# Step 1 to step 2 of the first batch by copies within SBUF for four of sixteen groups, and a new order of the prologue and the first chunk

## The chip, the core and the metric

One core of a Trainium2 chip. It has a matrix engine (TensorE, here PE, whose weight loads are shown as PEld), three others that compute (VectorE, DVE; ScalarE, ACT; GpSimd, POOL), SyncE (SP), which here only issues DMAs, and DMA engines that all queues share. SBUF is the memory on the chip, PSUM the one that PE writes to. The metric is the time of one execution on the device, in microseconds (us).

## The reference

```python
def reference(x, g_ln, w1, w2):                 # x: 8 x 3136 x 256
    x = np.fft.fft(np.fft.fft(x, axis=1), axis=2).real.astype(np.float32)
    mu = np.mean(x, axis=-1, keepdims=True)
    var = np.mean((x - mu) ** 2, axis=-1, keepdims=True)
    xn = (x - mu) / np.sqrt(var + 1e-06) * g_ln
    return x + np.maximum(xn @ w1, 0.0) @ w2    # w1: 256 x 1024, w2: 1024 x 256
```

The weights arrive as 64-bit floats, and the kernel reads them as pairs of 32-bit words.

## The kernel before

The Fourier transform over the 3136 positions of a batch is done in two steps, as 3136 = 64 x 49. Step 1 transforms over 64; the input is folded by symmetry, so that 25 of the 49 residues are left, which stand in 14 slots in two halves. Seven pieces i of two slots each pass through it: `load_x(b, i)`, `fold_zw` (DVE in the first batch), `step1` (PE, lines 247 and 249), a copy from PSUM to the tile `s1` (ACT, line 257). `s1` has the 64 results of both halves on its 128 partitions and slot, half and column in the free dimension. Step 2 contracts over the slots and eight of the partitions; so the data has to change its layout: `store1` (line 261) writes a piece to the tensor `scratch` in HBM, 256 KB each, and `relayout` (line 268) reads it back to the tile `s2` with slot and r on the partitions (8 x 14 = 112), and the 16 groups g (partition p = 16 r + g of `s1`) in the free dimension. In the trace `s1` and `s2` are both called s. `step2(m, ...)` (line 301) takes two groups of `s2` and the table `tab_s`, part "m" on PE; "h" and "f" are ACT's copies to the chunk's tiles (lines 321 and 323), "l" is DVE's low part (line 325).

What follows is done in 49 chunks c of 256 columns, each with 8 steps f of the hidden dimension, s = 8 c + f. `moe1_a(s)` multiplies with `w1` (six matmuls, line 345, three passes of high and low parts), which then already has the transform over the 256 columns in it; ACT copies one half (line 350), DVE makes both halves of h (lines 351 and 352). `moe1_b(s)` rounds h to its high part (ACT, line 359) and takes the rest as low part (DVE, line 360). `moe2(s)` multiplies with `w2` (twelve matmuls, line 395). `residual` (line 419) and its followers add x and the normalisation; `finish` (lines 468 and 470) and `store_out` write the result.

In the main loop, from s = 6 on, PE does `moe1_a(s)`, then `moe2(s - 3)`; `late` and `after` hold what else is due at a step, among it the folds, step 1 and the relayout of the next batch (in batch 1 the relayout is due after s = 34, its first step 2 after s = 45).

Before the loop stands a prologue whose order is written out by hand for PE, ACT, DVE, POOL and SP (lines 661 to 794). Beside step 1 of the first batch it makes the weights ready, in four quarters of each. For a quarter of w1: `convert_m` (DVE, lines 509 and 511), `convert_z` (ACT, line 517), `convert_b` (DVE, lines 522 and 524), `finish_w1` (DVE, line 552); then, for each half, `transform_w1` (PE, line 562, four matmuls to the profile for a call), `round_w1` (ACT, line 570), `rest_w1` (PE, line 575) and `rest_w1_copy` (ACT, line 580). For a quarter of w2, which is loaded to the place of the same quarter of w1 (`load_w2`): the same three conversions, `finish_w2` (DVE, line 584), and `split_w2`: the high part on ACT (line 528), the low part on POOL (line 529). `warm_up` runs matmuls on zeros.

Each engine does its instructions in order, and a wait of one holds all that stand behind it on that engine, DMA issues on its queue among them.

## Time and profile before

| | us |
|---|---|
| three timed runs | 1022.9, 1023.34, 1023.9 |
| their median | 1023.34 |
| profiled execution, its time | 1021.02 |
| profiled execution, its span | 1019.2 |

| engine | busy us in the span | share |
|---|---|---|
| PE | 1005.3 | 99% |
| DVE | 813.2 | 80% |
| ACT | 540.4 | 53% |
| POOL | 244.4 | 24% |

The span is from the first to the last instruction of the program; the time of that execution is 1.8 us longer. A row of the profile names the line of the kernel, the engine, the operation, the tiles (output <- inputs), the shapes, and in brackets the idle time of the engine before it and what ended that. A DMA row is the issue; its landing is told separately. PE's matmuls are pipelined, so the distance of two starts says what one costs.

### The profile page before, as it was taken

What the parts mean: (1) busy time and instruction counts of PE and PEld (TensorE: products, weight loads), DVE (VectorE), ACT (ScalarE), POOL (GpSimd) and SP (SyncE); (2) the same over time, 40 slices, a digit from 0 to 9 for tenths busy, and PEclk for the clock granted to TensorE, in tenths of its full rate; (3) what the DMA queues carried; (4) which work ended last, traced back from release to release, by engine and by line L of the source; (5) the groups of instructions that cost most, each with busy time, mean ns of one, the idle gap of its engine ahead of it and who ended that gap; (6) DMA issues with size and microseconds to landing.
All of it is one profiled execution on the core that took longest, in us unless ns stands there. A gap on an engine that the chain in (4) does not pass through costs nothing.

```text
span 1019.2 us, 21749 instructions
## 1 busy us (share of the span) xinstructions
PE 1005.3 (99%) x8279; PEld 984.7 (97%) x8280; DVE 813.2 (80%) x2190; ACT 540.4 (53%) x1416; POOL 244.4 (24%) x278
## 2 busy tenths in 40 slices
PE   9889999999999999999999999999999999999998
PEld 6779999999999999999999999999999999999998
DVE  7687887778787877878887887878788778878887
ACT  3545545655555455555456545555555554455453
POOL 2136504430154203341043401442024300000000
PEclk9999999999999999999999999999999999999999
DMA  9933343323222411243123132223101230100101
GB/s 348 265 129 105 105 125 104 103 74 104 74 83 94 146 52 53 85 135 104 43 89 119 66 105 81 83 94 122 56 30 46 73 104 23 42 22 22 43 22 42
DMA packets 41528, 92.10 MB, mean 90 GB/s; under 512 B 4176, under 2 KB 18704, under 8 KB 40528
## 3 DMA queue, kind: packets, MB, share of 16 engines
q1 hardware_dynamic: 40016, 88.87, 26.4%
q8 instruction: 66, 1.08, 0.4%
q0 software_dynamic: 320, 1.05, 0.3%
q10 hardware_dynamic: 1088, 0.79, 0.2%
q14 instruction: 38, 0.31, 0.1%
HBM read 50.32 MB, written 40.37 MB: 89 GB/s over the span
## 4 chain that ended last, share of the span: by engine, by line
PE 93%; DVE 4%; DMA 1%; ACT 1%; issue 0%; POOL 0%; SPq 0%; ACTq 0%; DVEq 0%
PE acc L395 52%; PE ab L345 26%; PE ps L301 5%; PE psy L419 4%; PE ps L254 3%; DVE h_lo L360 1%; PE ps L247 1%; PE ps L249 1%; DMA scratch<-s 1%; PE pw L659 1%; DVE h L351 1%; DVE h L352 1%; DMA s<-scratch 0%; ACT h_hi L359 0%; PE bb L345 0%
## 5 line engine op out<-in xcount | busy, mean ns | idle before, releaser
L395 PE MATMUL acc<-w_lo,h_hi 128*128 128x256 f32 x1568 | 438.5, 280 | 1.0 <-POOL w_lo L529 1.0
L395 PE MATMUL acc<-w_hi,h_lo 128*128 128x256 f32 x1568 | 438.5, 280 | 0.3 <-ACT w_hi L528 0.2
L395 PE MATMUL acc<-w_hi,h_hi 128*128 128x256 f32 x1568 | 438.6, 280 | 0.0
L360 DVE SCALAR_TENSOR_TENSOR h_lo<-h,h_hi 128x512 fp32r<-128x512 f32 x392 | 287.6, 734 | 173.3 <-ACT h_hi L359 171.4
L359 ACT ACTIVATE h_hi<-h 128x512 fp32r<-128x512 f32 x392 | 249.8, 637 | 259.6 <-DVE h L352 259.3
L395 PEld LDWEIGHTS acc<-w_lo,h_hi 128*128 128x128 f32 x1568 | 295.0, 188 | 1.2 <-POOL w_lo L529 1.2
L395 PEld LDWEIGHTS acc<-w_hi,h_lo 128*128 128x128 f32 x1568 | 295.3, 188 | 0.9 <-ACT w_hi L528 0.4
L395 PEld LDWEIGHTS acc<-w_hi,h_hi 128*128 128x128 f32 x1568 | 295.0, 188 | 0.0
L345 PE MATMUL ab<-ckl,w_hi 128*128 128x256 f32 x768 | 221.3, 288 | 2.3 <-DVE h L352 2.3
L345 PE MATMUL ab<-ckh,w_lo 128*128 128x256 f32 x768 | 216.7, 282 | 0.7 <-ACT w_lo L580 0.4
L345 PE MATMUL ab<-ckh,w_hi 128*128 128x256 f32 x768 | 215.5, 281 | 0.0
L217 POOL TENSOR_TENSOR fl<-f,fh 128x512 fp32r<-128x512 f32 x49 | 64.0, 1305 | 506.8 <-ACT fh L211 506.8
L351 DVE TENSOR_TENSOR h<-asb,ab 128x256 f32<-128x256 f32 x384 | 158.7, 413 | 1.9 <-ACT asb L350 1.9
L352 DVE TENSOR_TENSOR h<-asb,ab 128x256 f32<-128x256 f32 x384 | 158.7, 413 | 0.0
L345 PEld LDWEIGHTS ab<-ckl,w_hi 128*128 128x128 f32 x768 | 145.2, 189 | 6.2 <-issue 2.6
L350 ACT COPY asb<-ab 128x256 f32<-128x256 f32 x384 | 139.1, 362 | 19.8 <-PE ab L345 13.9
L345 PEld LDWEIGHTS ab<-ckh,w_lo 128*128 128x128 f32 x768 | 145.5, 189 | 3.3 <-ACT w_lo L580 0.6
L345 PEld LDWEIGHTS ab<-ckh,w_hi 128*128 128x128 f32 x768 | 145.7, 190 | 0.0
L321 ACT CAST ckh<-ps 128x392 fp32r<-128x392 f32 (+49 forms) x112 | 39.7, 356 | 66.6 <-PE ps L301 66.3
L257 ACT COPY s<-ps 128x508 f32<-128x508 f32 x56 | 32.7, 584 | 75.5 <-PE ps L254 62.5
L301 PE MATMUL ps<-tab_s,s 112*128 112x98 f32 (+1 forms) x512 | 65.6, 273 | 2.4 <-DMA s<-scratch 2.4
L301 PEld LDWEIGHTS ps<-tab_s,s 112*128 112x128 f32 x512 | 62.1, 192 | 2.9 <-issue 2.9
(108 smaller groups left out, 961.2 us busy)
## 6 DMA issues: line engine op xcount, KB each, us to landing
xs<-x SPq DMA_DIRECT2D x56, 512.0 KB, 4.3
out<-o SPq DMA_DIRECT2D x96, 256.0 KB, 2.4
scratch<-s SPq DMA_DIRECT2D x49, 256.0 KB, 2.1
s<-scratch SPq DMA_DIRECT2D x7, 1792.0 KB, 9.4
w1p_all<-w SPq DMA_DIRECT2D x8, 512.0 KB, 9.0
scratch<-s POOLq DMA_DIRECT2D x4, 256.0 KB, 6.4
s<-scratch SPq DMA_DIRECT2D x2, 448.0 KB, 5.4
s<-scratch SPq DMA_DIRECT2D x1, 896.0 KB, 12.1
```

The source lines that it names most:

```text
L217: nc.gpsimd.tensor_tensor(out=lo, in0=f, in1=hi.bitcast(F32), op=ALU.subtract)
L257: nc.scalar.copy(s[:, :, :, :127], ps[:, :, :, :127])
L301: nc.tensor.matmul(ps[:, h, k0 - base:k1 - base], s2[b][:KP, g, 128 * h:128 * h + 128], tab_s[:, h, k0:k1], start=(h == 0 and g == 2 * j), ...
L321: nc.scalar.copy(hi, src)
L345: nc.tensor.matmul(pt, wt[wi][:, j, fs], ch[xi][:, j, :w], start=(n == 0), stop=(n == 2))
L350: nc.scalar.copy(asb[:, :w], pa)
L351: nc.vector.tensor_tensor(out=h[:, :w], in0=asb[:, :w], in1=pb, op=ALU.add)
L352: nc.vector.tensor_tensor(out=h[:, w:], in0=asb[:, :m], in1=pb[:, :m], op=ALU.subtract)
L359: nc.scalar.activation(h_hi, h, AF.Relu)
L360: nc.vector.scalar_tensor_tensor(out=h_lo, in0=h, scalar=0.0, in1=h_hi.bitcast(F32), op0=ALU.max, op1=ALU.subtract)
L395: nc.tensor.matmul(acc[c, i][:, side], hs[xi][:, h0:h0 + 128], ws[wi][:, f], start=(f == 0 and side == 0 and n == 0), stop=(f == 7 and n = ...
L419: nc.tensor.matmul(ps[:, j, :129 + j], ck[:, j], ty_s[:, j, :129 + j], start=(j == 0), stop=True, skip_group_check=True)
```

## The change

Groups 0 to 3 of the first batch go from `s1` to `s2` by `direct`: for each group one DMA for the slots 0 to 9 (80 KB) and one for the slots 10 to 13 (32 KB), from eight partitions of `s1` to 80 or 32 of `s2`. For this the partitions of `s2` are ordered anew, in two parts with r outside and the slot inside, and the rows of the table `tab` with them; `relayout` becomes two DMAs, in all batches. The other twelve groups of the first batch and all later batches go by the scratch as before. The four copies of the first part are issued on POOL's queue after the last `ends`; the four of the second part in turn on ACT's and POOL's queue after the last `step1`. All stores of the first batch are issued by SP, after the loads of two quarters of w2. The relayout of the groups 0 to 3 and the warm-up ahead of step 2 are gone. `tw`, a part of `tab`, and `tz` are loaded earlier, w2 later. In the first chunk step 2 comes before the second half of w1 is transformed; the transform, its rounding and the conversions of w2 stand between the operations of the chunk, and `moe2` starts earlier in the order. The last quarter of w2 is converted in the steps 6 to 8 of the loop.

```diff
--- before.py
+++ after.py
@@ -39,6 +39,7 @@
 ROWS = NB * N
 NU = NS // 2
 KP = 8 * NS
+PARTS = (0, 10), (10, NS)
 
 
 def unit_k(unit):
@@ -94,7 +95,8 @@
                     else:
                         rows[:, 0, t:t + n], rows[:, 1, t:t + n] = ((c, s), (-s, c))[comp]
             t += n
-    tab = tab.transpose(3, 0, 1, 2, 4, 5).reshape(112, 2, HALF)
+    tab = tab.transpose(3, 0, 1, 2, 4, 5).reshape(NS, 8, 2, HALF)
+    tab = np.concatenate([tab[a:b].swapaxes(0, 1).reshape(-1, 2, HALF) for a, b in PARTS])
     tz = np.concatenate([tz.reshape(4 * NS, 50), np.zeros((KP - 4 * NS, 50))])
     d = np.arange(1, 129)[:, None]
     ang = 2 * np.pi * ((d * np.arange(129)) % D) / D
@@ -261,12 +263,21 @@
         in_order(eng.dma_start(scratch[b][2 * i:2 * i + 2].rearrange("s p d -> p s d"),
                                s.rearrange("p a h d -> p a (h d)")))
 
-    def relayout(b, g0=0, g1=16, eng=nc.sync):
+    def relayout(b, g0=0, g1=16):
         if b not in s2:
             s2[b] = work.tile([128, 16, D], F32, tag="s2", name=f"s2_{b}")
-        sv = scratch[b].rearrange("s (r g) d -> s r (g d)", g=16)
-        in_order(eng.dma_start(s2[b][:KP, g0:g1].rearrange("r g d -> r (g d)"),
-                               sv[:, :, g0 * D:g1 * D]))
+        sv = scratch[b].rearrange("s (r g) d -> r s (g d)", g=16)
+        for s0, e0 in PARTS:
+            in_order(nc.sync.dma_start(s2[b][8 * s0:8 * e0, g0:g1].rearrange("p g d -> p (g d)"),
+                                       sv[:, s0:e0, g0 * D:g1 * D]))
+
+    def direct(part, g0, g1, eng=nc.sync):
+
+        if 0 not in s2:
+            s2[0] = work.tile([128, 16, D], F32, tag="s2", name="s2_0")
+        s0, e0 = PARTS[part]
+        for g in range(g0, g1):
+            eng.dma_start(s2[0][8 * s0:8 * e0, g], s1[0][g:128:16, s0:e0])
 
     gb = group_bounds()
     chunk = {}
@@ -543,7 +554,7 @@
         nc.sync.dma_start(wp.rearrange("p (f d) -> p f d", f=2), w2v[:, 2 * n:2 * n + 2])
         w2p.append(wp)
 
-    gws = {}
+    gws, w2f = {}, []
 
     def finish_w1(n):
 
@@ -569,15 +580,13 @@
         for j in range(2):
             nc.scalar.copy(w1_cols(w1_hi, k, j), psw[k, j])
 
-    def rest_w1(k):
-
-        for j in range(2):
-            nc.tensor.matmul(psw[k, j], minus, w1_cols(w1_hi, k, j), start=False, stop=True,
-                             skip_group_check=True)
-
-    def rest_w1_copy(k):
-        for j in range(2):
-            nc.scalar.copy(w1_cols(w1_lo, k, j), psw.pop((k, j)))
+    def rest_w1(k, j):
+
+        nc.tensor.matmul(psw[k, j], minus, w1_cols(w1_hi, k, j), start=False, stop=True,
+                         skip_group_check=True)
+
+    def rest_w1_copy(k, j):
+        nc.scalar.copy(w1_cols(w1_lo, k, j), psw.pop((k, j)))
 
     def finish_w2(n):
         _, e, f = conv.pop(f"w2_{n}")
@@ -677,9 +686,11 @@
             load_w1(1)
             for i in (5, 6):
                 load_x(0, i)
+            nc.sync.dma_start(tw_all, tw)
             load_w1(2)
+            nc.sync.dma_start(tab_s[:, :, :gb[4]], tab[:, :, :gb[4]])
+            nc.sync.dma_start(tz_s, tz)
             load_w1(3)
-            nc.sync.dma_start(tw_all, tw)
             nc.gpsimd.memset(zmu, 0.0)
             nc.gpsimd.memset(masked, 0.0)
             ends(0, 0, 6)
@@ -693,12 +704,7 @@
             fold_zw(0, 2, nc.vector)
             step1(0, 2)
             convert_b("w1_0")
-            load_w2(0)
-            nc.sync.dma_start(tab_s[:, :, :gb[4]], tab[:, :, :gb[4]])
-            nc.sync.dma_start(tz_s, tz)
             step1_ends(0, 0, 6)
-            for i in range(3):
-                store1(0, i, nc.scalar if i % 2 else nc.gpsimd)
             ends(0, 6, 10)
             fold_zw(0, 3, nc.vector)
             step1(0, 3)
@@ -707,94 +713,105 @@
             step1(0, 4)
             finish_w1(0)
             step1_ends(0, 6, 10)
-            store1(0, 3, nc.scalar)
-            store1(0, 4, nc.gpsimd)
             ends(0, 10, NS)
+            direct(0, 0, 4, nc.gpsimd)
             convert_m("w1_1", w1p[1])
             fold_zw(0, 5, nc.vector)
             step1(0, 5)
             convert_z("w1_2", w1p[2])
             convert_b("w1_1")
+            load_w2(0)
             load_w2(1)
+            for i in range(5):
+                store1(0, i)
             fold_zw(0, 6, nc.vector)
             step1_ends(0, 10, NS)
-            store1(0, 5, nc.scalar)
+            store1(0, 5)
             step1(0, 6)
-            store1(0, 6, nc.gpsimd)
+            direct(1, 0, 1, nc.scalar)
+            direct(1, 1, 2, nc.gpsimd)
+            direct(1, 2, 3, nc.scalar)
+            direct(1, 3, 4, nc.gpsimd)
+            store1(0, 6)
             finish_w1(1)
+            nc.scalar.copy(minus, tw_all[:, 512:])
             convert_z("w1_3", w1p[3])
             convert_m("w1_2", w1p[2])
+            transform_w1(0, 0)
             convert_b("w1_2")
             finish_w1(2)
-            relayout(0, 0, 4)
-            relayout(0, 4, 8)
             load_w2(2)
             nc.sync.dma_start(tab_s[:, :, gb[4]:gb[8]], tab[:, :, gb[4]:gb[8]])
+            relayout(0, 4, 8)
             relayout(0, 8, 16)
-            nc.scalar.copy(minus, tw_all[:, 512:])
-            transform_w1(0, 0)
+            nc.sync.dma_start(ty_s, ty)
+            nc.sync.dma_start(tab_s[:, :, gb[8]:], tab[:, :, gb[8]:])
+            convert_m("w1_3", w1p[3])
+            convert_b("w1_3")
+            finish_w1(3)
+            load_w2(3)
+            for i in range(NU):
+                load_x(1, i)
             transform_w1(0, 1)
             round_w1(0)
-            convert_m("w1_3", w1p[3])
-            convert_b("w1_3")
-            load_w2(3)
-            nc.sync.dma_start(ty_s, ty)
-            nc.sync.dma_start(tab_s[:, :, gb[8]:], tab[:, :, gb[8]:])
-            for i in range(NU):
-                load_x(1, i)
-            finish_w1(3)
+            rest_w1(0, 0)
+            rest_w1_copy(0, 0)
+            convert_z("w2_0", w2p[0])
+            convert_m("w2_0", w2p[0])
+            convert_b("w2_0")
+            step2(0, "m")
+            rest_w1(0, 1)
+            step2(0, "h")
+            rest_w1_copy(0, 1)
+            step2(1, "m")
+            step2(0, "l")
+            f0 = finish_w2(0)
+            step2(1, "hl", 0)
+            convert_z("w2_1", w2p[1])
+            moe1_a(0, ((0, 0), (1, 0), (0, 1)))
+            moe1_a(1, ((0, 0), (1, 0), (0, 1)))
+            split_w2(0, f0)
             transform_w1(1, 0)
-            rest_w1(0)
-            convert_z("w2_0", w2p[0])
-            convert_z("w2_1", w2p[1])
-            rest_w1_copy(0)
+            convert_m("w2_1", w2p[1])
+            moe1_b(0)
+            step2(0, "f")
+            moe1_a(2)
+            moe1_b(1)
+            moe2(0)
             transform_w1(1, 1)
             round_w1(1)
-            convert_m("w2_0", w2p[0])
-            convert_b("w2_0")
-            f = finish_w2(0)
-            split_w2(0, f)
-            convert_m("w2_1", w2p[1])
             convert_b("w2_1")
-            warm_up(6, warm_h)
-            step2(0, "m")
-            step2(0, "hl")
-            step2(1, "m")
-            step2(1, "hl", 0)
-            f = finish_w2(1)
-            moe1_a(0, ((1, 0), (0, 0), (0, 1)))
-            split_w2(1, f)
-            step2(0, "f")
-            moe1_a(1, ((1, 0), (0, 0), (0, 1)))
-            rest_w1(1)
-            moe1_b(0)
-            moe1_a(2)
-            moe1_b(1)
+            moe1_a(3)
             moe1_b(2)
-            moe1_a(3)
-            rest_w1_copy(1)
+            f1 = finish_w2(1)
+            moe2(1)
+            rest_w1(1, 0)
+            rest_w1(1, 1)
+            split_w2(1, f1)
+            rest_w1_copy(1, 0)
+            rest_w1_copy(1, 1)
+            moe1_b(3)
+            step2(1, "hl", 1)
+            convert_a("w2_2", w2p[2])
+            moe1_a(4)
             step2(1, "f")
-            convert_a("w2_2", w2p[2])
-            step2(1, "hl", 1)
-            moe2(0)
-            moe1_b(3)
-            moe1_a(4)
+            moe2(2)
+            step2(2, "m")
+            moe1_b(4)
             convert_b("w2_2")
-            f = finish_w2(2)
-            split_w2(2, f)
+            f2 = finish_w2(2)
+            step2(2, "h")
+            moe1_a(5)
+            split_w2(2, f2)
+            step2(2, "l")
+            step2(2, "f")
             nc.gpsimd.tensor_scalar(out=neg, in0=ty_s[:, 1, 129:130], scalar1=2.0, scalar2=-1.0,
                                     op0=ALU.mult, op1=ALU.add)
-            moe2(1)
-            step2(2, "m")
-            moe1_b(4)
-            moe1_a(5)
-            step2(2, "hf")
-            step2(2, "l")
-            convert_a("w2_3", w2p[3])
-            moe2(2)
-            add_late(6, convert_b, "w2_3")
-            add_late(7, make_w2, 3)
-            add_late(8, split, t1_hi, t1_lo, tu_s[:, 0:128])
+            add_late(6, convert_a, "w2_3", w2p[3])
+            add_late(7, convert_b, "w2_3")
+            add_late(7, lambda: w2f.append(finish_w2(3)))
+            add_late(8, lambda: split_w2(3, w2f.pop()))
+            add_late(9, split, t1_hi, t1_lo, tu_s[:, 0:128])
 
         main.append(True)
         lag, last = 3, 8 * NCH
```

## Rows read from the trace of the kernel before

**Rows 1.** Windows: busy us (x instructions) by engine, granted clock, DMA share, GB/s.

```profile
28.90:33.20 4.30, 1.87 (x7) 0.59 (x6) 2.15 (x4) 3.14 (x6) 0.56 (x1) 1.00 0.88 228
33.20:39.40 6.20, 5.80 (x33) 5.52 (x34) 2.42 (x6) 2.65 (x8) 1.66 (x2) 0.72 1.07 265
...
48.20:60.00 11.80, 9.61 (x74) 8.71 (x73) 9.22 (x19) 7.12 (x20) 3.68 (x4) 1.00 0.61 241
...
100.00:1000.00 900.00, 899.12 (x7567) 892.08 (x7567) 722.45 (x1978) 485.79 (x1277) 209.23 (x231) 1.00 0.24 77
```

**Rows 2.** Timeline, 21 to 49 us: start, us, engine, line, names, idle before.

```profile
21.30 0.58 ACT L257 COPY s<-ps 128x508 f32<-128x508 f32 x1 [1.31 <-PE ps L249]
...
24.02 0.75 DVE L552 SCALAR_TENSOR_TENSOR gw<-fw,g_s,ew 128x512 f32<-128x512 f32 x1
...
28.31 0.80 SPq L268 DMA_DIRECT2D s<-scratch  x2
...
33.25 0.66 PE L301 MATMUL ps<-tab_s,s 112*128 112x99 f32 x4 [2.43 <-DMA s<-scratch]
...
35.82 0.57 PE L345 MATMUL ab<-ckh,w_lo 128*128 128x256 f32 x1 [0.35 <-ACT ckh L321]
...
48.20 0.29 PE L345 MATMUL ab<-ckl,w_hi 128*128 128x256 f32 x1
```

**Rows 3.** The chain of waits in order of time: start, us, what.

```profile
22.18 5.92 DMA scratch<-s
28.31 4.80 DMA s<-scratch
...
50.96 0.33 DVE h L351
```

**Rows 4.** Timeline of PE, 29 to 37 us: the warm-up, two matmuls of chunk 0.

```profile
29.58 1.24 PE L659 MATMUL pw<-warm_h 128*128 128x512 bf16 x5
...
36.40 0.41 PE L345 MATMUL ab<-ckl,w_hi 128*128 128x256 f32 x1
...
36.62 0.41 PE L345 MATMUL ab<-ckh,w_lo 128*128 128x256 f32 x1
```

**Rows 5.** DMA issues, whole run and (g_s) to 60 us: median to landing.

```profile
scratch<-s SPq DMA_DIRECT2D x49, 256.0 KB, 2.1
...
s<-scratch SPq DMA_DIRECT2D x7, 1792.0 KB, 9.4
...
g_s<-g_ln ACTq DMA_DIRECT2D x1, 1.0 KB, 3.6
```

**Rows 6.** Waits of SP's queue to 60 us: total, times, longest.

```profile
SPq L697 <- DMA scratch<-s: 5.9, 1, 5.9
```

**Rows 7.** Groups by line, 7 to 60 us: busy us, mean ns, idle before.

```profile
L562 PE MATMUL psw<-gw,tw_all 128*128 128x512 f32 x16 | 7.3, 599 | 0.7 <-DMA tw_all<-tw 0.7
...
L580 ACT CAST w_lo<-psw 128x512 fp32r<-128x512 f32 x4 | 2.1, 588 | 0.0
...
L350 ACT COPY asb<-ab 128x256 f32<-128x256 f32 x9 | 3.3, 367 | 2.4 <-PE ab L345 2.4
...
L524 DVE SCALAR_TENSOR_TENSOR ew<-w1p_all,ew 128x512 int32<-128x512 int32 x8 | 5.5, 692 | 0.3
...
L522 DVE TENSOR_SCALAR ew<-ew 128x512 int32<-128x512 int32 x8 | 3.4, 422 | 1.3 <-ACT ew L517 1.3
...
L529 POOL TENSOR_TENSOR w_lo<-fw,w_hi 128x512 fp32r<-128x512 f32 x4 | 5.1, 1286 | 30.8 <-ACT w_hi L528 30.8
```

**Rows 8.** Line 360 from 40 to 75 us: shortest, median, longest in ns.

```profile
L360 DVE SCALAR_TENSOR_TENSOR h_lo<-h,h_hi x13: 678/684/1367, 39.8 to 73.0; 128x512 fp32r<-128x512 f32 x13
```

**Rows 9.** Waits from 48.2 to 73.6 us: total, times, longest.

```profile
PE ab L345 <- DVE h L352: 1.4, 4, 0.6
...
PE psy L419 <- DVE o L470: 1.3, 1, 1.3
...
PE acc L395 <- POOL w_lo L529: 1.0, 1, 1.0
```

## The prediction

> **What bounds the kernel now.** I read the time by stretch first. From 100 to 1000 us TensorE (PE) is busy 899.12 of 900 us with 7567 matmuls at the full granted clock, 0.119 us each [rows 1]: nothing that this change touches can shorten that part. What is left to win lies in front of it, where PE is busy only 1.87 of 4.30 us (28.9 to 33.2) and 9.61 of 11.80 us (48.2 to 60.0), and where the granted clock is 0.72 between 33.2 and 39.4 [rows 1]. PE's work is the same in both kernels but for the warm-up; so the end moves by what PE loses there: idle time, warm-up and half clock. Second, the timeline around 28.9: PE's first step-2 matmul (line 301) starts at 33.25 after an idle 2.43 us "<-DMA s<-scratch" [rows 2]. Third, the chain of waits says where that comes from: the last store to the scratch takes 5.92 us from 22.18, the relayout 4.80 us from 28.31 [rows 3]. The last step-1 copy on ACT has ended at 21.88 (21.30 + 0.58) [rows 2]; so 11.4 us lie between the last result of step 1 and the first matmul of step 2, and 10.7 of them are two DMAs in a row.
>
> **The change, part by part.**
>
> Removed: for groups 0 to 3, store and relayout as a chain; the first relayout (448 KB); the warm-up of six bf16 matmuls ahead of step 2 (five of them are 1.24 us [rows 4], so some 1.4). Added: eight copies SBUF to SBUF, four of 80 KB (pairs 0 to 4) on GpSimd's queue, long before they are needed, and four of 32 KB (the last pairs), two on ACT's queue and two on GpSimd's, once ACT has copied the last pair.
>
> **When the copies land.** Groups 0 and 1 need one copy from ACT and one from GpSimd, issued at about 22.0. No row shows a copy within SBUF. The nearest: a store of 256 KB lands 2.1 us after its issue in the middle of the kernel, with quiet queues, and 1 KB on ACT's queue in the busy prologue takes 3.6 us [rows 5]; the store at 22.18, in the same traffic, took 5.92 [rows 3]. The copy is small like the 3.6 us one and stands in the same kind of traffic, so I take 3.6: **landed at 25.6**, with ends 24.1 and 27.9. Then everything but PE has to be ready too. PE's own part before step 2 (eight transform matmuls of 0.46 us, from 7.3 us for 16 [rows 7], one cast and one rest matmul) ends at about 25.0, since the table tw is now loaded two places earlier and no longer waited for (0.7 us [rows 7]). So landing before 25.0 wins nothing more.
>
> **From there to chunk 0.** In the trace the first matmul of chunk 0 (line 345, 35.82) comes 2.57 us after the first of step 2 (33.25) [rows 2]. The new order puts one rest matmul and one w_lo cast (mean 0.59 [rows 7]) between; some 0.4 of it shows: 25.6 + 3.0 = 28.6. VectorE (DVE) must have the low part ready: the last quarter of w1 ends at 24.77 (24.02 + 0.75) [rows 2], ACT's two DMA issues and the later order of its scalings push that by up to 0.75 to 25.5; the first quarter of w2 takes 2 x (0.42 + 0.69) = 2.2 [rows 7], the low part 0.5, finish_w2 0.7: 28.9, so PE waits another 0.3 for it. DVE is therefore the second bound, level with the copies.
>
> **The first chunk, in the new order.** moe1_a(0) and (1): 12 x 0.119 = 1.4, to 30.3. ACT's copy 0.37 [rows 7] and DVE's two halves of h at 0.33 [rows 3]: 31.4. The integer half of w2's second quarter, now ahead of h_lo(0), 1.1: 32.5; h_lo(0) 0.68 [rows 8]: 33.2. Here I add a collision. GpSimd's low part of w2 (1.29 us each [rows 7]) falls into this stretch now. In the trace h_lo takes 0.684 at the median and 1.367 at the most [rows 8], double when it meets that GpSimd operation. I count one such doubling, 0.68: moe2(0) starts at 33.9. The Trainium skill (SBUF — State Buffer, Who interferes with whom) says that a VectorE instruction with two SBUF inputs and a GpSimd instruction that reads SBUF exclude each other for a whole instruction; by it this part of the order pays what I count, and without the collision the sum would be 0.7 lower. PE then does moe2(0) 1.4, four transform matmuls 1.8, moe1_a(3) 0.7: 37.9. moe1_a(4) waits for w_lo of w1's second half, and that stands on ACT behind w2's second quarter: ACT's copy 0.4, h(3) 0.7, h_lo(2) 0.7, finish_w2(1) 0.7, w_hi 0.6, w_lo twice 0.6 = 4.3, to 42.2; moe2(1) and the rest matmuls (1.4 + 0.5) hide in it, some 2 us of PE's wait are new. Then half of moe1_a(4) 0.4, moe2(2) 1.4, step 2 of the third piece 1.0, moe1_a(5) 0.7: **moe1_a(6) starts at 45.7**. In the trace it starts at 48.20 [rows 2]: 2.5 us earlier.
>
> So of 7.6 us won at step 2, five are given back: 0.4 and 0.3 before chunk 0, the rest because DVE and ACT still have w2 to convert, and conversions that ran in the wait for the relayout before now stand between the chunk's operations.
>
> **After that** the same work follows, except that all of w2's last quarter comes later (steps 6 to 8). PE's waits from 48.2 to 73.6 are 1.4 for DVE's h, 1.0 for GpSimd's low part of that quarter, 1.3 for DVE's output [rows 9]. Later conversion can lengthen the first two by up to 0.7; equally the 1.3 can go if DVE has more room at that place. I take nothing, with -1.3 and +0.7 as ends.
>
> **Costed at nothing.** The scratch stores move to SP's queue behind two w2 loads; needed only for groups 4 and up, whose step 2 starts at about 44, some 15 us after they can have landed; w2, tables and the next batch's x queue behind them with at least as much room. If that cover were gone, each us of delay would show. The relayouts of all later batches become two DMAs each in another row order; one takes 9.4 us today [rows 5], and even twice that fits: batch 1's relayout is issued after step 34 and read in step 45, 11 steps of 18 matmuls, 11 x 2.1 = 23 us. On GpSimd six issues take the place of four; it has nothing due until w2's low part at about 31. On ACT two issues take the place of three, but now stand ahead of `minus`, the scaling of w1's last quarter, the casts and all of chunk 0: their 0.75 is counted above.
>
> **Sum.** -2.5 us. The profiled execution spans 1019.2 us in a run of 1021.02; it would become 1016.7 and 1018.5. The three timed runs lie 2.3 us higher, at a median of 1023.34; I set the difference on it: **1020.8 us**. The bounds: a landing at 25.0 instead of 25.6 gives 0.6 and no collision 0.7, but then DVE is late, so together some 1.2; with the 1.3 gone, -5.0: 1018.3. A landing at 27.9 costs 2.3, a later quarter 0.7, half clock 1.2 (below): +1.7 with all of these, 1025.0.
>
> **Rivals.**
>
> (a) The copies are late. Against the sum, every us of landing after about 25.3 is a us of the end, as PE and DVE wait there and nothing fills in. At 27.9 (5.92 after 22.0) the gain is 0.2: 1023.1. For it: the store at 22.18 was that late, and in the new order SP has two w2 loads and six stores queued beside the copies. Against: they are eight times smaller. The Trainium skill (DMA: Bandwidth & Descriptors, Why a DMA increments its semaphore by 16 and not by 1) says that the number of DMA engines is the largest up to 16 that divides the slowest dimension of both sides; the source has 8 partitions, so by it each copy would run on 8 engines. No row here shows such a copy; by that rule the later end is the likelier one.
>
> (b) Half clock. In the trace PE ran idle for 2.43 us and then at half clock: matmuls 0.22 us apart at 36.40 and 36.62 [rows 4], granted clock 0.72 [rows 1], in spite of the warm-up. With PE idle for 0.6 us before step 2 it should stay; from a landing at about 27.4 on (2.4 us idle) it falls again, and moe1_a(0) and (1) cost 12 x 0.1 = 1.2 more: with (a), 1024.3.
>
> (c) The queue holds ACT: slower. SP's load of tab waited 5.9 us for a scratch store that it doesn't read [rows 6]: a DMA issue can be held until an earlier DMA has landed. The last copies now stand on ACT behind loads and stores of SP, and ACT is in order: if its first issue is held for a store (the last landed at 28.1 in the trace [rows 3]), scaling, casts and step 2 all start from there. Landing 28.1 + 3.6 = 31.7, 6.1 later: -2.5 + 6.1 = +3.6, 1026.9. It decides from an issue held beyond about 26.5, where the sum turns to +2. Against: by the written order the DMAs a few places ahead of it are loads of w1 and of tables, not stores.
>
> (d) The change doesn't do what it says, since step 2's other inputs (tables, w1) are late instead: then chunk 0 starts as in the trace and the order costs what it adds; between 1022 and 1026.
>
> **Chances.** Forecast 0.58, (a) with (b) 0.25, (c) 0.1, (d) 0.07. The range takes in the forecast's bounds and (a) with (b): 1018.3 to 1025.0. Runs tell 0.2%, 2.05 us, from no change: faster than 1021.3 needs the landing before about 26. From the forecast 0.53 is faster and 0.05 within; (a) is mostly within, at its earliest faster, at its latest slower; (c) slower: faster 0.56, same 0.29, slower 0.15.
>
> **What would show it.** Right: line 301 starts at 25 to 26.2, line 345 at 28 to 29.2, moe1_a(6) at 45 to 46.5, no stretch of low clock, a wait of PE for w_lo (line 580) of 1.5 to 2 us near 40, one h_lo or conversion of DVE near 32 of double length. Wrong: line 301 after 27; ACT idle between 21.9 and 23 at a DMA issue; PE waits from 48 to 74 well away from 3.9 us; any PE idle between 100 and 1000 us beyond 0.9.

## The result and the profile after

The kernel after takes **1024.53 us** (median of 22 runs, 1023.36 to 1026.09), the kernel before beside it 1023.32 (22 runs): the ratio is 1.0021, 95% interval 1.0013 to 1.0029. It is slower by 0.2%, where 1020.8 and faster was forecast. The time lies inside the range, at its upper end, where the rivals (a) and (b) together stood (1024.3). That this number nearly fits is in part luck: these two rivals add up to +1.0 us, and the two profiled executions lie 4.4 us apart.

The profiled execution after spans 1023.6 us in a run of 1025.42. TensorE by stretches (columns: stretch, its length, busy time of PE, weight loads, DVE, ACT, GpSimd with instruction counts, granted clock, DMA share, GB/s), to be read beside [rows 1]:

```profile
core 0: us, PE busy (x) PEld busy (x) DVE busy (x) ACT busy (x) POOL busy (x), PEclk, DMA share, GB/s
...
25.00:29.00 4.00, 1.58 (x5) 0.61 (x4) 2.38 (x5) 2.98 (x6) 0.00 (x0) 0.89 0.66 207
29.00:33.00 4.00, 4.00 (x19) 3.82 (x18) 2.71 (x5) 1.06 (x2) 0.00 (x0) 0.50 0.91 260
33.00:39.00 6.00, 5.65 (x18) 3.93 (x17) 3.14 (x6) 3.05 (x8) 1.29 (x1) 0.55 0.78 249
39.00:48.00 9.00, 7.01 (x44) 5.47 (x42) 5.67 (x12) 3.94 (x8) 0.27 (x1) 1.00 1.02 224
...
60.00:78.00 18.00, 15.53 (x115) 14.95 (x114) 16.92 (x41) 7.86 (x20) 9.52 (x12) 0.91 0.13 45
...
104.00:1000.00 896.00, 895.17 (x7534) 888.18 (x7533) 717.99 (x1965) 483.95 (x1271) 209.87 (x231) 1.00 0.24 77
```

The long part is untouched: 895.17 busy of 896. The loss is in front. PE is busy only 1.58 of 4 us up to 29, and then, busy without a gap, runs at a clock of 0.50 and 0.55 (1.2 GHz of 2.4 nearly throughout) up to 39; in the kernel before that stretch is 33.2 to 39.4 alone, at 0.72 [rows 1].

PE's timeline of the kernel after (start, duration, engine, line, operation, in brackets the idle time before it and what ended it); line 301 of before is 312 now, 345 is 356, 395 is 406:

```profile
27.01 0.19 PEld L585 LDWEIGHTS psw<-w_hi,minus 128*128 128x128 f32 x1 [2.15 <-ACT w_hi L581]
27.01 0.50 PE L585 MATMUL psw<-w_hi,minus 128*128 128x512 f32 x1 [1.32 <-DMA s<-s]
...
28.61 1.15 PE L312 MATMUL ps<-tab_s,s 112*128 112x99 f32 x4 [1.10 <-issue]
...
33.52 0.58 PE L356 MATMUL ab<-ckh,w_hi 128*128 128x256 f32 x1 [0.35 <-ACT ckh L332]
...
40.42 0.39 PE L406 MATMUL acc<-w_hi,h_lo 128*128 128x256 f32 x1 [0.54 <-DVE h_lo L371]
...
48.19 0.38 PE L356 MATMUL ab<-ckh,w_lo 128*128 128x256 f32 x1 [1.65 <-ACT w_lo L589]
...
52.17 0.36 PE L356 MATMUL ab<-ckl,w_hi 128*128 128x256 f32 x1
...
63.80 0.38 PE L406 MATMUL acc<-w_hi,h_lo 128*128 128x256 f32 x1 [1.40 <-ACT w_hi L539]
...
65.16 0.39 PE L406 MATMUL acc<-w_lo,h_hi 128*128 128x256 f32 x1 [0.98 <-POOL w_lo L540]
```

Step 2 starts at 28.61 (33.25 in [rows 2]; forecast 25.6), moe1_a(0) at 33.52 (35.82; 28.6), moe1_a(6) at 52.17 (48.20; 45.7). The lead of 4.6 us at step 2 is 2.3 at moe1_a(0) and a lag of 4.0 at moe1_a(6). The first two rows are one matmul, the first rest of w1's transform. It doesn't read a copy of s; the row of its weight load names what it waited for, ACT's cast w_hi. The other engines' rows of the timeline, and the copies' rows of the DMA issues (count, size, median us to landing):

```profile
18.78 11.18 SPq L263 DMA_DIRECT2D scratch<-s  x7
...
22.82 2.76 ACTq L280 DMA_DIRECT2D s<-s  x2
25.62 0.30 ACT L737 CAST minus<-tw_all 128x128 fp32r<-128x128 f32 x1 [2.83 <-issue]
...
26.51 0.43 DVE L533 TENSOR_SCALAR ew<-ew 128x512 int32<-128x512 int32 x1 [2.48 <-ACT ew L528]
...
37.46 1.29 POOL L540 TENSOR_TENSOR w_lo<-fw,w_hi 128x512 fp32r<-128x512 f32 x1 [13.30 <-ACT w_hi L539]
...
37.56 1.47 DVE L520 TENSOR_SCALAR mw<-w1p_all 128x512 int32<-128x512 int32 x1
```
```profile
s<-s POOLq DMA_DIRECT2D x4, 80.0 KB, 6.1
...
s<-s POOLq DMA_DIRECT2D x2, 32.0 KB, 5.0
```

ACT spends 2.76 us on two DMA issues; `minus` waits 2.83 for that, DVE 2.48 for ACT's next scaling; the cast w_hi stands behind these on ACT, so PE's first idle stretch (1.32) comes from ACT's hold. GpSimd's two late copies (groups 1 and 3) take 5.0 us to land. The first matmul of step 2 reads group 0, whose last copy ACT issues; the views give no landing for it. In the trace the last update of that copy's semaphore comes at 28.52, 5.70 after the start of its issue and 0.09 before step 2, and the first packet of ACT's queue behind that issue moves only at 26.10.

**Profiles and medians differ here.** The two profiled executions lie 4.4 us apart, the medians 1.2. Executions of one kernel spread, and in the kernel before the time goes with the mean granted clock that each reports. Of 35 executions of before in one series, 9 ran at 0.998 (mean 1020.84), 4 at 0.996 (1022.96), 20 at 0.995 (1024.47). Its profile is one at 0.998. The 22 of after ran at 0.992 to 0.997; the 8 at 0.993 took 1025.28 on average, the 6 at 0.997 1024.16. The Trainium skill (TensorE: Matmul & The Clock Gate, Part 1) says that the number of matmuls at low clock varies between runs of one kernel; the runs agree. So a profile is used below for links of the chain, and the ratios for what a change is worth.

### The profile page after: what moved, and what is told of

Its sections match the earlier page's. It is cut to its first block, busy times and chain, and to the rows that moved or that the text cites. A ratio compares the mean times of both kernels' runs of the same rounds, so it can differ in the third digit from the quotient of the medians.

```text
span 1023.6 us, 21771 instructions
## 1 busy us (share of the span) xinstructions
PE 1009.5 (99%) x8274; PEld 988.2 (97%) x8274; DVE 813.2 (79%) x2190; ACT 541.6 (53%) x1416; POOL 244.5 (24%) x280
## 4 chain that ended last, share of the span: by engine, by line
PE 95%; DVE 2%; issue 1%; ACT 1%; DMA 0%; POOL 0%; POOLq 0%; ACTq 0%; DVEq 0%
PE acc L406 52%; PE ab L356 26%; PE ps L312 6%; PE psy L430 4%; PE ps L256 3%; PE pw L668 1%; PE ps L249 1%; DVE h_lo L371 1%; PE ps L251 1%; DMA s<-s 0%; DVE h L362 0%; DVE h L363 0%; POOL w_lo L540 0%; ACT h_hi L370 0%; PE bb L356 0%
```

## The experiments

The profiles of all kernels, cut at the same points: end of ACT's last copy of step 1, then what was added up to the start of step 2, moe1_a(0), moe1_a(6) and moe1_a(14). From moe1_a(14) to moe1_a(380) all take 907.2 to 907.4 us. "Forecast" is the sum on record, put in the same way.

| kernel | copy ends | to step 2 | to moe1_a(0) | to moe1_a(6) | to moe1_a(14) |
|---|---|---|---|---|---|
| before | 21.89 | 11.36 | 2.57 | 12.38 | 25.37 |
| before, again (e9) | 21.78 | 11.47 | 2.57 | 12.22 | 25.37 |
| before, 16 warm-ups (e8) | 22.96 | 12.18 | 2.57 | 11.46 | 25.38 |
| forecast | 21.88 | 3.7 | 3.0 | 17.1 | 25.4 |
| after | 22.79 | 5.82 | 4.91 | 18.65 | 26.19 |
| after, again (e10) | 22.29 | 7.08 | 4.08 | 18.62 | 27.38 |
| late quarter early (e4) | 22.52 | 6.78 | 3.50 | 18.63 | 26.43 |
| warm-ups (e1) | 21.96 | 6.62 | 2.81 | 17.66 | 26.14 |
| stores and load behind (e2) | 21.88 | 3.67 | 3.55 | 24.65 | 24.34 |
| stores behind (e5) | 22.76 | 4.21 | 3.15 | 19.46 | 24.70 |
| same, warm-ups (e6) | 22.08 | 5.58 | 2.84 | 17.63 | 25.93 |
| stores behind, SyncE copies (e11) | 21.85 | 4.34 | 2.81 | 17.63 | 26.19 |
| same, late quarter early (e13) | 22.83 | 3.11 | 2.81 | 18.30 | 26.95 |
| copies in the old order (e3) | 22.00 | 9.63 | 3.54 | 12.77 | 26.21 |
| same, stores behind (e7) | 22.52 | 8.15 | 2.60 | 11.79 | 26.49 |
| same, loads moved (e12) | 22.52 | 8.14 | 2.60 | 11.84 | 26.07 |
| same, no warm-up (e14) | 21.60 | 6.71 | 2.50 | 15.01 | 25.57 |

The first column moves by 1.4 us between kernels that do much the same up to there, so a start in one profile says little below 1 us.

**e1: warm-ups in the idle stretch.** The theory: the half clock is a loss by itself, on top of the late landing.

```diff
+            warm_up(6, warm_h)
             rest_w1(0, 0)
...
+            warm_up(5, warm_h)
             step2(0, "m")
```


> The changed kernel with warm-up matmuls in PE's wait for the copies: six ahead of the first rest_w1, five ahead of step 2. Half-clock theory: PE's wait (2.9 us between 25.7 and 28.6 in the changed kernel's profile) is what brings half clock from 28 to 38.6; with it filled the clock stays at 1.0, line 312 starts at 28.7 as before, moe1_a(0) at about 31.8 (33.5 in the changed kernel), moe2(0) at about 37 (40.4), and the time falls by 3 us to about 1021.5. Rival, the copies' landing or the order of the chunk is what costs: the clock matters little since DVE and ACT are the bound, and the time falls by under 0.7 us, 1024.

Measured: 1022.39, ratio 0.9999 (0.999 to 1.0009). The windows of e1:

```profile
25.00:29.00 4.00, 2.89 (x16) 1.35 (x15) 3.68 (x7) 1.84 (x4) 0.00 (x0) 1.00 0.81 277
29.00:33.00 4.00, 3.65 (x29) 3.25 (x28) 1.36 (x3) 2.16 (x5) 0.00 (x0) 1.00 0.96 301
33.00:39.00 6.00, 4.46 (x26) 3.30 (x26) 5.88 (x12) 2.78 (x8) 1.29 (x1) 1.00 0.77 203
```

Clock 1.00 in all three; step 2 is as late as in the kernel after (28.58 against 28.61), but the next two links shrink from 4.91 and 18.65 to 2.81 and 17.66. The low clock costs 3.1 us of the profile and 2.2 by the ratios: that is as much as the whole difference between the kernel after and the one before. It leaves no gain, and step 2 as late as it was.

**e2: stores and w2's second load behind the copies.**

```diff
-            load_w2(1)
-            for i in range(5):
-                store1(0, i)
...
-            store1(0, 5)
...
-            store1(0, 6)
+            for i in (6, 0, 1, 2, 3, 4, 5):
+                store1(0, i)
+            load_w2(1)
```


> The changed kernel with SP's stores of the first batch and the second w2 load moved behind the copies in the order: SP issues the store of piece 6 first, so that none of them starts before the last step-1 copy. Traffic theory (SP's stores and loads in front hold ACT's two issues at 1.2 and 1.5 us and GpSimd's copies at 5 us to landing): ACT's issues take 0.4 us each, GpSimd's copies for groups 1 and 3 land at about 26 instead of 28.1 and 28.6, line 312 starts at about 26.3, the half clock is gone or short, and the time falls by 3 to 5 us to 1019.5 to 1021.5. Rival, the copies are slow by themselves (eight partitions, rows of 1 KB): they still land some 5 us after issue, line 312 starts at 28 or later, time within 0.7 us of 1024.5.

Measured: 1025.76, ratio 1.0031 (1.0021 to 1.0041). The DMA row of the late copies and one of ACT's timeline in e2:

```profile
s<-s POOLq DMA_DIRECT2D x2, 32.0 KB, 3.4
```
```profile
33.48 0.66 ACT L528 ACTIVATE ew<-w1p_all 128x512 f32<-128x512 f32 x1 [4.43 <-DMA w1p_all<-w]
```

The copies land in 3.4 us and step 2 starts at 25.55, before the 26.3 of the theory, though ACT's two issues still take 1.87; but I had moved w2's load too, and ACT waits 4.43 us for it: moe1_a(0) to (6) takes 24.65. The edit was two changes in one, and only its first half tells something.

**e3: the copies alone, in the order of before.** Prologue and first chunk are those of before; only the relayout of groups 0 to 3 is replaced by the eight copies.

```diff
             ends(0, 10, NS)
+            direct(0, 0, 4, nc.gpsimd)
...
+            direct(1, 0, 1, nc.scalar)
+            direct(1, 1, 2, nc.gpsimd)
+            direct(1, 2, 3, nc.scalar)
+            direct(1, 3, 4, nc.gpsimd)
             store1(0, 6, nc.gpsimd)
...
-            relayout(0, 0, 4)
```


> The kernel before with the path alone: groups 0 to 3 by the eight copies (first part on GpSimd after the last ends, second part on ACT and GpSimd after the last step 1, ahead of the last store), no relayout of these groups, everything else in the old order, stores on ACT and GpSimd as before. Order theory (the path is good and the new order loses): PE is through with the transforms and the warm-up at 30.9 and the copies have landed by then, so step 2 starts at about 31 instead of 33.25, without a wait and without half clock; 2 to 4 us faster than before, 1019.5 to 1021.5. Path theory (the copies land late in the prologue's traffic whatever the order): step 2 at 32 or later, within 1 us of before, 1022.3 to 1024.

Measured: 1021.43, ratio 0.9988 (0.9977 to 0.9999). ACT's timeline in e3:

```profile
22.03 3.50 ACTq L280 DMA_DIRECT2D s<-s  x2
25.58 0.69 ACT L528 ACTIVATE ew<-w1p_all 128x512 f32<-128x512 f32 x1 [3.58 <-issue]
...
31.45 0.68 ACT L528 ACTIVATE ew<-w1p_all 128x512 f32<-128x512 f32 x1 [3.47 <-DMA w1p_all<-w]
```

The time is what the order theory said, step 2 (31.63) a little later. It follows PE's own warm-up without idle time, when the copies have long landed (GpSimd's at 28.9 and 29.1): 1.7 us are won there. ACT's hold of 3.5 pushes the last quarter of w1's transform back, to 28.29 from 27.65, and ACT's wait of 3.47 for a load stands ahead of moe1_a(0), 3.54 after step 2 instead of 2.57; 0.3 is left at moe1_a(6).

**e4: w2's last quarter converted where it was.**

```diff
-            add_late(6, convert_a, "w2_3", w2p[3])
-            add_late(7, convert_b, "w2_3")
+            convert_a("w2_3", w2p[3])
+            add_late(6, convert_b, "w2_3")
+            add_late(7, make_w2, 3)
```


> The changed kernel with the last quarter of w2 converted as in the kernel before (both first halves ahead of the loop, then steps 6 and 7, the split of t1 in step 8). If the late conversion costs: PE's waits before moe2(6), 1.4 and 1.0 us, become 0.2 and 1.0, the half clock at 65 to 69 us is gone, and the time falls by 1.2 to 2 us, 1022.5 to 1023.3. Rival, that wait is caught up in the slack behind it (the distance to the kernel before goes from 6.3 us at moe1_a(13) to 4.8 at moe1_a(14)): under 0.5 us.

Measured: 1024.95, ratio 1.0024 (1.0013 to 1.0035): no gain. PE's wait of 1.40 us for that quarter's `w_hi` falls to 0.21, and moe1_a(14) still starts at 77.86 (78.36 after): PE waits 1.3 for DVE's output there, which it doesn't after, and 1.9 instead of 0.8 for h. The theory that the late quarter makes the kernel slower falls.

```profile
62.48 0.38 PE L406 MATMUL acc<-w_hi,h_lo 128*128 128x256 f32 x1 [0.21 <-ACT w_hi L539]
```

**e5: only the stores behind the copies.** e2 without its flaw: w2's load stays early.

```diff
-            for i in range(5):
-                store1(0, i)
...
-            store1(0, 5)
...
-            store1(0, 6)
+            for i in (6, 0, 1, 2, 3, 4, 5):
+                store1(0, i)
```


> The kernel after the change, with one thing moved: SyncE issues the seven stores to the scratch behind the eight copies (the one of groups 12 to 15's last piece first), while the load of w2's second quarter stays as early as it is. Theory (the copies land late because the stores' bytes are in flight beside them, and everything up to moe1_a(6) is late for that): GpSimd's last copy lands at 25.5 to 26.5 instead of 28.6, the transform's second step starts at 26 to 27 instead of 28.61, moe1_a(0) at 29 to 30 instead of 33.52, TensorE's idle stretch shrinks below 1.5 us and most of the half clock between 28 and 38 goes; the time is 2 to 4 us under that of the kernel after, 1020.5 to 1022.5. Rival (the start doesn't matter, the loss is in the reordered conversions behind it): moe1_a(0) is early in the same way, but moe1_a(6) stays at 51 to 52 and the time within 0.7 us of 1024.5. A second rival (ScalarE is held by its own two DMA issues whatever else is in flight): the issues still take 1.2 to 1.5 us each and the step starts at 28 or later, 1024.

Measured: 1021.33, ratio 0.9983 (0.9972 to 0.9993), 3.9 us under the kernel after by the ratios. The DMA row and ACT's issues in e5:

```profile
s<-s POOLq DMA_DIRECT2D x2, 32.0 KB, 3.7
```
```profile
22.79 1.85 ACTq L280 DMA_DIRECT2D s<-s  x2
```

Landing 3.7 instead of 5.0, ACT held 1.85 instead of 2.76, step 2 at 26.97. In the table step 2 follows the last copy of step 1 by 5.82 to 7.08 in the four profiles with the stores ahead, by 3.11 to 5.58 in the five with them behind (5.58 is e6, where the warm-ups hold it). Group 0's last copy shows it more clearly, by its semaphore as above: from the start of its issue it takes 5.70, 6.96, 6.66 and 6.35 us in after, e10, e4 and e1, and 3.29, 4.09, 4.52, 4.23 and 3.00 in e2, e5, e6, e11 and e13. In after, e10, e4, e5, e11 and e13 step 2 starts 0.09 us behind that update. So the stores in front make the copy late, and the copy holds step 2. They are not all of it: in the old order, with the stores behind, GpSimd's two copies still take 5.4, 5.7 and 6.2 us (e7, e12, e14) and group 0's 4.5 to 5.7.

**e6: e5 with the warm-ups of e1.**

> The stores behind the copies as in the run above, and eleven warm-up matmuls in TensorE's idle stretch (six ahead of the rest of w1's transform, five ahead of step 2), so that the clock doesn't fall. Theory (late copies and half clock are separate losses that add): granted clock 1.00 from 25 to 39, moe1_a(0) at 29 to 29.5, moe1_a(6) at 46.5 to 47.5, 1 to 2 us under the run above: 1019.5 to 1021. Rival (w2's conversions set moe1_a(6), not moe1_a(0)): the chunks start early but wait as much longer for w_lo and w_hi, moe1_a(6) at 48 or later, the time within 0.7 us of the run above.

Measured: 1021.95, ratio 0.999 (0.9978 to 1.0002): nothing beyond e5. PE in e6:

```profile
26.34 1.25 PE L668 MATMUL pw<-warm_h 128*128 128x512 bf16 x5
27.65 0.69 PE L312 MATMUL ps<-tab_s,s 112*128 112x99 f32 x4
```

With the full clock moe1_a(0) to (6) takes 17.63, as in e1; the rival's longer waits there don't show, though its time does. But step 2 follows the warm-ups without idle time, while group 0's copy had landed at 26.63: the warm-ups themselves cost up to 0.9 us at step 2 (0.3 at group 1, whose copy landed at 27.95). GpSimd's two copies took 5.5 us in that execution although the queues were those of e5 (3.7). In e5 itself the clock was 1.00 up to 39 already, so there was little left to win in that stretch.

**e7: the old order, the copies, the stores behind them.**

```diff
-            for i in range(3):
-                store1(0, i, nc.scalar if i % 2 else nc.gpsimd)
...
-            store1(0, 6, nc.gpsimd)
+            for i in (6, 0, 1, 2, 3, 4, 5):
+                store1(0, i)
```


> The order of the kernel before for the prologue and the first chunk, with the eight copies in place of the way by the scratch for groups 0 to 3 and all stores behind the copies on SyncE. Theory (the path is good once the stores are out of its way, and the order of before fills TensorE until the copies land): TensorE has the whole of the transform of w1 until about 28.3, step 2 starts at 28.3 to 29 without a half-clock stretch, moe1_a(0) at 31.5 to 32.5 instead of 35.82, moe1_a(6) at 46 to 47 instead of 48.20; 1019 to 1021.5. Rival (moe1_a(6) waits for w2's conversions, whose times the path doesn't move): moe1_a(0) early, moe1_a(6) at 47.5 to 48.5, the time within 0.7 us of 1022.5 to 1023.3. Second rival (ScalarE's issues, 1.2 to 2.3 us each, push the conversions of w1 and w2 back by as much): moe1_a(6) at 49 or later and 1024.

Measured: 1019.81, ratio 0.997 (0.9956 to 0.9983). PE has the transform of w1 until about 29.2, the copies land meanwhile, no low clock up to 39; moe1_a(6) starts at 45.06, 3.1 earlier than before. Step 2 itself (30.67) and moe1_a(0) (33.27) come later than the theory said, behind PE's own transform and its six warm-ups. One us of the 3.1 goes again at

```profile
50.21 1.16 PE L430 MATMUL psy<-ty_s,ck 128*128 128x129 f32 x8 [2.92 <-DMA ty_s<-ty]
```

where a table's load, queued late on SyncE, ends PE's wait.

**e8: the kernel before with 16 warm-up matmuls instead of 6.**

> The kernel before with sixteen instead of six warm-up matmuls ahead of the transform's second step, and nothing else: measures what the half clock at its 35.9 to 39.3 costs. Theory (half clock in this stretch costs about half of its length): granted clock 1.00 there, moe1_a(6) 1 to 1.7 us earlier, 1021.5 to 1022.3. Rival (the step behind it waits for w2's conversions): clock 1.00, but moe1_a(6) within 0.5 us of 48.20 and the time within 0.5 us of that of before.

Measured: 1021.00, ratio 0.9983 (0.9971 to 0.9994). The window in e8 (0.74 in before, by the same cut):

```profile
33.00:39.00 6.00, 3.72 (x29) 3.35 (x29) 1.45 (x3) 1.43 (x4) 1.25 (x1) 1.00 1.07 272
```
```profile
35.14 0.66 PE L301 MATMUL ps<-tab_s,s 112*128 112x99 f32 x4 [1.93 <-DMA s<-scratch]
```

9 of its 12 executions ran at 1.000. Ten more warm-ups are worth 1.7 us in the kernel before, as much as e5 wins: a gain that has nothing to do with the path. Where it arises the profile doesn't show. moe1_a(0) to (6) is 0.9 shorter, but step 2 comes 0.8 later after the last copy of step 1, as it waits for the relayout, and moe1_a(6) starts at 49.18, not at 47.2 or earlier as the theory had it.

**e9 and e10: both kernels once more.**

> The kernel before, unchanged, for a second profile: how far do the points of the prologue move between executions of one program? Its profiled execution took 1021.02 where its median over many is 1022.5 to 1023.8. Theory (executions differ by when the loads and the relayout land): the relayout's landing, and so step 2's start (33.25 in the first profile), moves by up to 2 us, moe1_a(6) (48.20) by 0.5 to 1.5, and the span with it. Rival (the prologue repeats to some tenths of a us, the spread comes later): step 2's start within 0.3 us of 33.25, and the difference of the spans shows behind 100 us.

> The kernel after the change, unchanged, for a second profile. Theory: GpSimd's last copy lands at 28 to 29 again, step 2 starts at 28 to 29.2, half clock from there to about 38, moe1_a(6) at 51 to 53, the span 1022 to 1024. Rival (the first profile was an outlier, with ScalarE's two issues of 1.2 and 1.5 us by chance): step 2 at 25.5 to 27, no half clock, moe1_a(6) at 49 or earlier, the span 1020 or less.

Measured: 1020.9 (span 1019.1) and 1026.48 (span 1024.7). PE in e9, then ACT's issues and the DMA row in e10:

```profile
33.25 0.66 PE L301 MATMUL ps<-tab_s,s 112*128 112x99 f32 x4 [2.51 <-DMA s<-scratch]
...
35.82 0.58 PE L345 MATMUL ab<-ckh,w_lo 128*128 128x256 f32 x1 [0.35 <-ACT ckh L321]
```
```profile
22.32 3.38 ACTq L280 DMA_DIRECT2D s<-s  x2
```
```profile
s<-s POOLq DMA_DIRECT2D x2, 32.0 KB, 6.4
```

Before repeats to 0.2 us, and again at a clock of 0.998; what its longer executions look like no profile shows. After repeats in kind: copies still later (6.4), step 2 at 29.37, a clock of 0.66 from 29 to 39. The first profile was no outlier.

**e11: e5 with the four last copies on SyncE.** ScalarE issues none.

```diff
-            direct(1, 0, 1, nc.scalar)
-            direct(1, 1, 2, nc.gpsimd)
-            direct(1, 2, 3, nc.scalar)
-            direct(1, 3, 4, nc.gpsimd)
+            direct(1, 0, 4)
```


> The stores behind the copies as before in this series (ScalarE's two issues took 1.85 us there and step 2 started at 26.97), and the four copies of the last pairs issued by SyncE, one after the other, so that ScalarE and GpSimd issue none of them. Theory (the landing of the copies sets step 2): SyncE issues from 22.2 to 24, the last lands at 27 to 27.5, step 2 at 26.9 to 27.8, the time within 0.7 us of 1021.3. Rival (ScalarE's hold sets it, by delaying the cast of w1 and the rest matmul ahead of step 2): ScalarE's cast of minus at 22.8 instead of 24.68, step 2 at 25 to 26, moe1_a(0) at 28 to 28.8 instead of 30.12, 1 to 1.5 us less: 1020.

Measured: 1020.54, ratio 0.9973 (0.9961 to 0.9985). SyncE's and PE's timeline in e11, and a window:

```profile
21.87 2.73 SPq L280 DMA_DIRECT2D s<-s  x4
...
24.65 5.40 SPq L263 DMA_DIRECT2D scratch<-s  x7
```
```profile
26.19 0.66 PE L312 MATMUL ps<-tab_s,s 112*128 112x99 f32 x4 [1.13 <-issue]
...
29.00 0.39 PE L356 MATMUL ab<-ckh,w_hi 128*128 128x256 f32 x1 [0.35 <-ACT ckh L332]
...
46.62 0.36 PE L356 MATMUL ab<-ckl,w_hi 128*128 128x256 f32 x1
...
58.24 0.39 PE L406 MATMUL acc<-w_hi,h_lo 128*128 128x256 f32 x1 [1.41 <-ACT w_hi L539]
```
```profile
60.00:62.00 2.00, 2.00 (x12) 2.00 (x12) 1.94 (x6) 0.63 (x1) 1.92 (x4) 0.53 0.00 0
```

This is the kernel that the forecast described: 26.19, 29.00 and 46.62 against 25.6, 28.6 and 45.7, and by the ratio 2.8 us are won where 2.5 were forecast. Its interval lies clear of that of e1, where the clock was full too and the copies late; so the landing costs time beyond the clock. The size has a caveat: by the profiled executions (spans of 1018.5 and 1019.2) only 0.7 us are won, and the twelve executions, all from 1020.17 to 1020.97, stand where the faster ones of before stand. That ScalarE's hold by itself matters for step 2 is not shown: counted from the last copy of step 1 it follows after 4.34 (e13: 3.11) with SyncE issuing, 3.67 and 4.21 with ScalarE (e2, e5), and the intervals of the ratio of e5 and e11 overlap. Behind moe1_a(6) 0.8 is given back; the waits for w2's last quarter and low clock from 60 on stand there.

**e12: e7 with two loads moved on SyncE** (ty with the first tables, w2's third quarter ahead of the relayout).

> The order of before with the eight copies and the stores behind them, and two places changed on SyncE's queue: the table ty is loaded with the first tables (its late load held TensorE for 2.92 us at 50.2), and w2's third quarter with its table ahead of the first relayout (SyncE stood there until 31.36 for the stores). Theory (the gain of 3.1 us that moe1_a(6) has in that order is lost at 50 to that load and to the late third and last quarters of w2): no wait of TensorE for ty, moe1_a(7) at 48 to 49.5 instead of 51.12, and 0.5 to 2 us less in the end: 1018 to 1019.3. Rival (w2's last quarter lands at about 49 whatever the order, and the chunk waits for that): the wait turns into one of the same length for w_hi or w_lo, the time within 0.5 us of 1019.8.

Measured: 1019.46, ratio 0.9967 (0.9952 to 0.9981). The wait for ty is gone, the lead of 3.1 us holds up to moe1_a(12); of the span 0.3 us is left, less than the runs can tell.

**e13: e11 with w2's last quarter converted where it was** (the edit of e4).

> The kernel with the stores behind the copies and SyncE's copies (1020.54), and the last quarter of w2 converted where it was before the change, ahead of the chunks' steps 6 to 8 instead of in them. Theory (the late quarter costs what is missing at the end): TensorE's waits for w_hi and w_lo of that quarter near 58 and 59.6 fall from 1.41 and 0.98 to 0.2 and 1.0 as in the kernel before, no half clock at 62 to 66, and the end is 0.8 to 1.6 us earlier: 1019 to 1019.8. Rival (VectorE has the same work either way, and the earlier conversion pushes h of steps 6 and 7): moe1_a(6) or (7) later by as much, the time within 0.5 us of 1020.54.

Measured: 1021.95, ratio 0.999 (0.9979 to 1.0001). PE's waits in e13:

```profile
54.59 0.36 PE L356 MATMUL ab<-ckl,w_hi 128*128 128x256 f32 x1 [0.87 <-DVE h L363]
...
58.08 0.38 PE L406 MATMUL acc<-w_hi,h_lo 128*128 128x256 f32 x1 [0.22 <-ACT w_hi L539]
```

The wait for `w_hi` goes, one for DVE's `h` takes its place, and the kernel is 1.4 us slower than e11 by the medians (the intervals overlap a little). The rival holds as to the mechanism: what PE doesn't wait for there it waits for here, 2.4 in all for h (0.7 in e11) and 1.3 for DVE's output. With neither the wait for `w_hi` nor low clock (1.00 from 60 to 78) moe1_a(6) to (14) takes 26.95, longer than in e11. The later quarter isn't a cause of the loss.

**e14: e12 without its warm-up.**

```diff
-            warm_up(6, warm_h)
             step2(0, "m")
```


> The order of before with the copies, the stores behind them and the two loads moved (1019.46), without the six warm-up matmuls (1.46 us) ahead of step 2. Theory (TensorE's own work sets moe1_a(0) there): step 2 at 29.2 instead of 30.7, moe1_a(0) at 31.8 instead of 33.26, 1 to 1.4 us less: 1018 to 1018.5. Rival (VectorE, busy with w2's conversions up to 34.4 in that kernel, sets the first h): moe1_a(0) starts up to 1.4 earlier but waits for the low part ckl and for h, moe1_a(6) within 0.4 us of 45.1, the time within 0.5 us of 1019.46.

Measured: 1019.03, ratio 0.9958 (0.9942 to 0.9974), the best of all beside e12, whose interval it overlaps. PE's timeline and a window in e14:

```profile
30.81 0.39 PE L356 MATMUL ab<-ckh,w_lo 128*128 128x256 f32 x1 [0.35 <-ACT ckh L332]
...
33.22 0.58 PE L356 MATMUL ab<-ckl,w_hi 128*128 128x256 f32 x1 [1.91 <-DVE ckl L336]
```
```profile
33.00:39.00 6.00, 5.79 (x25) 5.59 (x26) 3.52 (x9) 3.08 (x8) 1.30 (x1) 0.50 0.81 226
```

moe1_a(0) starts 2.45 us earlier than in e12 (0.9 of it is step 1) and then PE waits 1.91 for DVE's low part; after that wait the clock is 0.50 and moe1_a(6) is 0.7 later than in e12. In this order DVE's conversions hold the first chunk, not PE: the rival, on the profile, with the low clock on top.

## Why the prediction was wrong

**The step that failed is the landing of the copies.** I took 3.6 us because the copy is small like one 3.6 us row, with 5.92 (the store at 22.18, in the same stretch [rows 3]) as the far end. Group 0's copy, on which step 2 waited, took 5.70, and 6.35 to 6.96 in e10, e4 and e1; GpSimd's two took 5.0, 6.4, 6.3 and 5.6 there. The row of the same stretch was the right neighbour, and the row of the same size the wrong one. Nor does that row stand "in the same kind of traffic": in the kernel before it was issued at 0.75 us, where 125 GB/s moved, and from 22 to 28 it was 334.

```profile
0.75 0.46 ACTq L669 DMA_DIRECT2D g_s<-g_ln  x1
```
```profile
0.70:4.40 3.70, 2.90 (x4) 1.36 (x5) 0.82 (x3) 1.49 (x2) 0.33 (x2) 1.00 0.54 125
22.00:28.00 6.00, 6.00 (x15) 2.88 (x16) 4.81 (x9) 2.39 (x5) 0.75 (x1) 1.00 0.92 334
```

With the stores out of the way 3.0 to 4.5 was measured for group 0 in the same order of the chunk, and e5 is 3.9 us faster than after: the stores ahead of the copies made them late. What the engine-count rule that the prediction cited costs can't be judged: no run took the traffic away and left the shape.

**A second term was mis-sized:** ACT's two issues, "0.75 us" by the issues of stores in the trace, took 2.76 (3.38 in e10, 3.50 in e3; 1.83 to 1.88 in e1, e2, e5, e6, e7 and e12). With it, and with the 0.9 us that step 1 ran later, PE's own part ahead of step 2 ended at 27.5, not at 25.0, and 1.0 before the copy landed: an earlier landing alone could have won no more than that at step 2. Rival (c) as told, an issue held until a store has landed, decides from 26.5 and did not occur: both issues were over at 25.58.

**Half clock** was rival (b), with the right place and too small a price. PE idles 1.32 + 1.10 = 2.42 us, and the low clock lasts not over moe1_a(0) and (1) alone (1.2) but to 38: 3.1 on the profile (after against e1: 2.1 + 1.0), 2.2 by the ratios.

The rest of the sum was nearly right. Step 2 to moe1_a(0): 3.0 forecast, 2.8 at full clock (e1, e6, e11, e13; 3.15 and 3.55 in e5 and e2, where PE first waits for group 2). moe1_a(0) to (6): 17.1 against 17.6 at full clock (e1, e6, e11). 0.4 of the 0.5 is the collision: not `h_lo` was doubled (0.68 counted) but the integer half ahead of it, `mw` at 37.56, 1.47 instead of 0.42 beside GpSimd's 1.29. The Trainium skill (SBUF — State Buffer, Who interferes with whom) has the two engines exclude each other for a whole instruction; the trace agrees, but the condition that the prediction quoted, two inputs from SBUF, was too narrow: `mw` has one. PE's wait for `w_lo` is 1.65 (1.5 to 2 forecast). After moe1_a(6) I took nothing with -1.3 and +0.7; it was +0.8: the wait for DVE's output did go, one of 1.4 for w2's last quarter came, and a second stretch of low clock (0.91 from 60 to 78). Which of these makes the 0.8 isn't shown, as e13 has neither of the last two and is no shorter there.

**The sum, closed.** Forecast -2.5, profile +4.8 at moe1_a(14): 7.3 off. By the table: 0.9 step 1 itself, 2.1 the landing with ACT's hold, 1.9 and 1.55 the clock and the chain, 0.8 behind; together 7.25. In the medians it is 3.7 off, since the profile of before is one of its shorter executions, 2.3 under its median, and that of after one of its longer, 0.9 above; I had seen the first and not asked why.

**On path and order.** That the order gives back most of what the path wins was right: moe1_a(0) to (6) takes 17.6 to 18.3 in the new order at full clock and 11.5 to 12.8 in the old one (15.0 in e14, which starts earliest). What I had not weighed is the other combination. In the old order PE has work until the copies land whatever they take; 3.1 us reach moe1_a(6) (e7, e12), and e12 is no slower than e11. By the profiles, too, only the kernels in the old order lie clearly under before (spans of 1016.5 to 1016.8 in e7, e12 and e14 against 1019.2; 1018.5 to 1019.5 in e5, e6 and e11). The reordering isn't what the path needed.

**Still open:** which stretches carry the low clock in the executions of before that no profile shows; why the same queues gave 3.7 us in e5 and 5.5 in e6, and what else is in the copies' way in the old order; and what holds ACT's second issue (0.6 to 2.3 us).

## What to carry to other kernels

Price a DMA by the row nearest to it in time and traffic, not in size, and count the issue itself where an engine with work behind it has to make it. A reordering that moves filler work out of a wait bets on the landing: ask what TensorE does if the transfer is 2 us late, and count the clock that it loses by then, up to the end of the low stretch. Before a sum is set on a profile, look where that execution lies among the kernel's runs and at its granted clock.
